# Attention and two feed-forward layers: the first batch pair in three full passes, opening loads in order of use, weights narrowed by an integer add

## The chip, the core and the metric

The kernel runs on one core of a Trainium2 chip. A core has five engines that run beside each other: TensorE (PE, matrix products; PEld is its weight load), VectorE (DVE), ScalarE (ACT), GpSimd (POOL) and SyncE (SP), which here issues all DMAs in order. The metric is the device time of one launch in microseconds.

## The reference

The inputs are eight batches of eight heads, 576 tokens, head size 64, and 32 packed queries per head; the weights come as 64-bit floats, which reach the kernel as pairs of 32-bit words.

```python
p_packed = sm_attn(p, k, v)               # 32 packed rows per head
out = sm_attn(q, p_packed, p_packed)      # every token against the 32 rows
x = out.transpose(0, 2, 1, 3).reshape(4608, 512)
xn = x / sqrt(mean(x * x) + 1e-6) * rms_g
x = (silu(xn @ w_gate) * (xn @ w_val)) @ w_out          # 1536 wide
h = x @ w_in
out = (max(h, 0) + alpha * min(h, 0)) @ w_out2          # 2048 wide
```

## The kernel before

**Products.** Every large product is made of three TensorE products of rounded parts (`mm3`, L107 to L110): high by high, high by low, low by high. The parts are made by `split_hi` on ScalarE (L96) and `split_lo` on VectorE (L99), or on GpSimd for output weights in later passes (L314).

**First feed-forward layer.** Its gate and value weights are folded with the packed values of a batch: `wg_job(b, j)` (L649) makes for batch b the folded weights of 256 hidden columns, six jobs a batch. A pass takes one chunk of tokens through the hidden blocks f of 128 columns: `blk_in` for gate and value (12 products per cut of the chunk between batches, two times six), silu (L886), product (L892), split (`hsplit`), then one step later `blk_out` (12 products into four PSUM banks that hold y). At the end of the pass y goes to DRAM (L930, L931).

**Chunks.** Batches 2 to 7 are taken in pairs: 320 tokens, 512 tokens (256 of either batch), 320 tokens. Batches 0 and 1 are taken in chunks of 320, 256, 320 and 256, and the two of batch 0 in half passes: first half of the blocks for both chunks, then second half, with partial y written out (`part`), reloaded (L874) and added (L923). Each half pass and each pass is an entry of `PASSES`; `NEWQ` and `XNEXT` say which chunk's queries are worked on and taken over in it.

**Narrowing.** The weights of the first layer are 36 units: 24 of gate and value columns, 12 of output rows, half a megabyte each. A unit is loaded wide by SP (L194 four DMAs, L199 one), then narrowed from 64 to 32 bits by `narrow`: shift and mask (L213, VectorE), sign and exponent bits (L220, VectorE), the low word as a float scaled by 2^-52 (L218, ScalarE), the exponent alone (L224, VectorE), their product (L228, GpSimd, or L231 on VectorE), and a float add (L239, GpSimd, or L237 on VectorE for the second layer's units, which `conv_late` narrows during the later passes). Narrowed gate and value units are also written to DRAM (L250), from where later batches reload them (L637). Eight wide buffers serve the first 18 units, four the rest. The generator `conv_all` narrows two units at a time; `conv` takes some of its steps and `conv_to(n)` takes all up to unit n.

**Attention.** `k_steps(b)` is the key chain of a batch: 11 TensorE steps, with evacuations between, that end in the packed values (`ppbd`, `ppB`, `ppG`). `q_steps` takes up to 256 query tokens: transposes (L537), scores (L553), softmax on VectorE and ScalarE (L564 to L583), a product whose squares give the norm (L590, L599), the power on GpSimd (L604), and the scaling (L613). Its scores need `ppB` of the batch. `x_split` makes the parts xh and xl that `blk_in` reads.

**Order.** The kernel writes the order of every engine's work by hand. In a step f: gate block, `work(f, 1)`, value block, `work(f, 2)`, `burst(f)`, `work(f, 3)`, then `blk_out(f - 1)` and the split of the next output weights. `burst` has four slots: folding jobs listed in `JOBS` take two each, key and query chains take what their step says. `work` runs the chains' evacuations; softmax steps with an exponential only at the third place, with table loads around (L353). In the passes of batch 0 and the half passes `work` also takes two narrowing steps; in later passes it takes steps of `conv_late`. At the end of a pass all steps of the next chunk's queries that are left are issued in one go, ahead of the last two `blk_out`. The prologue (from L664 on) loads keys and values, then weights and queries, runs the first key chain and the first query chains, narrows four units and folds the first job.

Of the kernel before, what the change touches and what calls it, by code (L numbers as in the profile page):

```python
# [18 lines left out]
def attention_moe_moe2_kernel(ctx, tc, q, k, v, p, w_gate, w_val, w_out, rms_g, w_in2, w_out2, alpha, out):  # L19
# [19 lines left out]
    NQ = 3  # L39
# [4 lines left out]
    CH = [(0, 320, [(0, 320, 0)]), (320, 256, [(0, 256, 0)]), (576, 320, [(0, 320, 1)]), (896, 256, [(0, 256, 1)])]  # L44
    for b in range(2, B, 2):
        t0 = b * S
        CH.append((t0, 320, [(0, 320, b)]))
        CH.append((t0 + 320, 512, [(0, 256, b), (256, 512, b + 1)]))
        CH.append((t0 + 832, 320, [(0, 320, b + 1)]))
    tiles, of_chunk = [], []  # L50
    for t0, n, _ in CH:
        ids = []
        for o in range(0, n, 128):
            ids.append(len(tiles))
            tiles.append((t0 + o, min(128, n - o)))
        of_chunk.append([ids[i:i + 2] for i in range(0, len(ids), 2)])
    HF = NF // 2
    PASSES = [(0, 0, HF), (1, 0, HF), (0, HF, NF), (1, HF, NF)] + [(c, 0, NF) for c in range(2, len(CH))]

    NEWQ = {0: 1, 2: 2, 4: 3, 5: 4}  # L60
    XNEXT = {0: 1, 3: 2, 4: 3, 5: 4}
    JOBS = {0: {1: [(0, 1)], 3: [(0, 2)]}, 1: {5: [(0, 3)]}, 2: {7: [(0, 4)], 9: [(0, 5)]}, 3: {11: [(1, 0)]},
            4: {2 * j + 1: [(1, j + 1)] for j in range(5)}, 5: {2 * j + 1: [(2, j)] for j in range(6)}}
    for i in range(6, len(PASSES)):
        b = 2 + (i - 6) // 3 * 2
        if i < len(PASSES) - 1:
            NEWQ[i] = XNEXT[i] = i - 1
        if (i - 6) % 3 == 0:
            JOBS[i] = {11: [(b + 1, 0)]}
        elif (i - 6) % 3 == 1:  # L70
# [41 lines left out]
    with tc.manual_schedule():  # L112
# [96 lines left out]
        def narrow(t, w, pool, late=False):  # L209
            lo, hi = t[:, :, :, 0], t[:, :, :, 1]  # L210
            wi = w.bitcast(I32)
            r = lo.bitcast(F32)
# [4 lines left out]
            if pool:  # L217
                nc.scalar.activation(out=r, in_=lo.bitcast(U32), func=ACTF.Copy, scale=2.0 ** -52)  # L218
# [4 lines left out]
            yield  # L223
            nc.vector.tensor_scalar(  # L224
                out=hi, in0=wi, scalar1=-0x800000, scalar2=None, op0=ALU.bitwise_and
            )
            if pool:
                nc.gpsimd.tensor_tensor(out=r, in0=r, in1=hi.bitcast(F32), op=ALU.mult)  # L228
            else:
                yield  # L230
                nc.vector.scalar_tensor_tensor(  # L231
                    out=r, in0=lo.bitcast(U32), scalar=2.0 ** -52, in1=hi.bitcast(F32),
                    op0=ALU.mult, op1=ALU.mult,
                )
            if late:
                yield
                nc.vector.tensor_tensor(out=w, in0=w, in1=r, op=ALU.add)  # L237
            else:
                nc.gpsimd.tensor_tensor(out=w, in0=w, in1=r, op=ALU.add)  # L239

        def conv_unit(n, pool):
# [5 lines left out]
            yield from narrow(staged.pop(n), w, pool)  # L247
# [5 lines left out]
        def conv_late():  # L253
            ahead = [load_wide(u, one, NST) for u in units2[:2]]
            for i, u in enumerate(units2):
                w = one.tile([128, 4, 128], F32, tag="w32", name="w32", bufs=2)
                yield from narrow(ahead.pop(0), w, 0, True)
# [16 lines left out]
        def conv_all():  # L274
            while n_conv[0] < NU1:
# [4 lines left out]
                live = [conv_unit(n, 1), conv_unit(n + 1, 1 if n % 3 else 0)]  # L280
# [62 lines left out]
        q_open = {b: sum(tiles[ids[0]][0] // S == b for c in of_chunk for ids in c) for b in range(B)}  # L343
# [281 lines left out]
        def new_x():  # L625
            return (one.tile([128, G, S], F32R, tag="xh", name="xh"),
                    one.tile([128, G, S], F32R, tag="xl", name="xl"))
# [71 lines left out]
        nc.sync.dma_start(out=g_col.rearrange("p (c o) -> p c o", o=1)[0:D], in_=rms_g[0:256].rearrange("(c d o) -> d c o", d=D, o=1))  # L699
        nc.sync.dma_start(out=g_col.rearrange("p (c o) -> p c o", o=1)[D:2 * D], in_=rms_g[256:512].rearrange("(c d o) -> d c o", d=D, o=1))  # L700
# [7 lines left out]
        nc.sync.dma_start(out=alpha_sb, in_=alpha.rearrange("(f p) -> p f", p=128))  # L708
        qa.run()
        warmup(3)  # L710
        qb = Chain(q_steps((2,), bk_pro), 0)
        qb.run()
        conv(1)
        warmup(3)
        qb.run()
        conv(1)
        qa.run()
        warmup(3)
        qb.run()
# [4 lines left out]
        qb.run()  # L724
# [3 lines left out]
        for i in range(2):  # L728
            x_split(of_chunk[0][i], xh, xl, i * 256)
# [44 lines left out]

        for i_p, (c, f0, f1) in enumerate(PASSES):
            last = i_p == len(PASSES) - 1
            t0, n, cuts = CH[c]
            xo = 320 * (c == 1)
            steady[0] = i_p > 3
            if i_p == 1:  # L780
                chains["k"] = [Chain(k_steps(b, bk_at), b) for b in range(1, B)]
# [240 lines left out]
```

## Time and profile before

| | us |
|---|---|
| median of 3 runs | 1797.76 (1795.12 to 1803.67) |
| the profiled execution | 1799.78 |
| its span, first to last instruction | 1798.0 |
| TensorE busy | 1680.2 (93%) |
| VectorE busy | 1112.8 (62%) |
| ScalarE busy | 820.4 (46%) |
| GpSimd busy | 282.2 (16%) |

The profile takes one execution apart. Busy times are sums per engine; TensorE's products are pipelined, so their durations overlap and the distance from start to start says more than the duration of one. The ends of the passes can be read from the instructions that take y out of PSUM: 135.0, 169.6, 210.0 and 246.3 us for the half passes, 318.5 and 384.5 for the two chunks of batch 1, then 451.1, 537.9 and 604.1 for the next pair. The second feed-forward layer begins at about 994.

### The profile page before, as it was taken

How to read it: one execution, taken by the hardware profiler on the slowest of the kernel's cores; microseconds unless marked ns; L12 is line 12 of the kernel's file. 1: busy time of each engine (PE TensorE's matmuls, PEld its weight loads, DVE VectorE, ACT ScalarE, POOL GpSimd, SP SyncE). 2: the span in 40 equal slices, each digit the busy share in tenths (PEclk: the TensorE clock that was granted, in tenths of full speed). 3: DMA queues.
4: the chain of work that ended last, by engine and by line, in shares of the span. 5: the costliest groups of instructions: out<-in, count | busy, mean ns of one | idle time of the engine just before them, and what ended most of it. 6: DMA issues, size and time to landing. Idle time of an engine off the chain costs nothing.

```text
span 1798.0 us, 27195 instructions
## 1 busy us (share of the span) xinstructions
PE 1680.2 (93%) x10448; PEld 1390.7 (77%) x10448; DVE 1112.8 (62%) x1945; ACT 820.4 (46%) x1564; POOL 282.2 (16%) x232
## 2 busy tenths in 40 slices
PE   6567879889999899999999999999999999999999
PEld 5256658678887798888889788888888888888887
DVE  3797747666646765566533666666666666666665
ACT  3236556666547655465545333333333333333332
POOL 1654202222222222233223000000000000000000
PEclk7779989999999999999999999999999999999999
DMA  8736636663545543443206101010101010100000
GB/s 191 211 124 191 184 105 188 178 184 92 145 140 156 159 121 114 141 154 100 91 24 229 68 1 48 1 48 0 48 0 48 0 48 0 47 1 24 1 24 24
DMA packets 163426, 164.05 MB, mean 91 GB/s; under 512 B 88544, under 2 KB 110048, under 8 KB 163296
## 3 DMA queue, kind: packets, MB, share of 16 engines
q1 hardware_dynamic: 163296, 162.32, 30.1%
q8 instruction: 82, 1.34, 0.3%
q14 instruction: 48, 0.39, 0.1%
HBM read 127.54 MB, written 34.73 MB: 90 GB/s over the span
## 4 chain that ended last, share of the span: by engine, by line
PE 78%; DVE 7%; ACT 7%; DMA 2%; issue 2%; SPq 1%; POOL 1%; DVEq 0%; ACTq 0%; POOLq 0%
PE ps_y L108 12%; PE ps_y L109 12%; PE ps_y L110 12%; PE ps_g L109 10%; PE ps_g L110 10%; PE ps_g L108 10%; PE ps_v L108 2%; PE ps_v L110 2%; PE ps_v L109 2%; PE ps_wg L649 2%; PE ps_at L590 1%; ACT L353 1%; DVE s L892 1%; ACT in_h L96 1%; ACT hh L96 1%
## 5 line engine op out<-in xcount | busy, mean ns | idle before, releaser
L96 ACT ACTIVATE hh<-s2m 128x512 fp32r<-128x512 f32 x144 | 91.1, 633 | 495.8 <-DVE s2m L975 495.8
L96 ACT ACTIVATE in_h<-w_raw 128x512 fp32r<-128x512 f32 x354 | 221.5, 626 | 113.1 <-PE ps_y L109 96.5
L314 POOL TENSOR_TENSOR in_l<-w_raw,in_h 128x512 fp32r<-128x512 f32 x131 | 177.9, 1358 | 559.1 <-ACT in_h L96 498.6
L109 PE MATMUL ps_g<-yl,in_h 128*128 128x512 f32 x576 | 228.0, 396 | 0.0
L110 PE MATMUL ps_y<-in_h,hl 128*128 128x512 f32 x576 | 226.9, 394 | 0.0
L109 PE MATMUL ps_y<-in_l,hh 128*128 128x512 f32 x576 | 226.8, 394 | 0.0
L110 PE MATMUL ps_g<-yh,in_l 128*128 128x512 f32 x576 | 226.4, 393 | 0.0
L108 PE MATMUL ps_y<-in_h,hh 128*128 128x512 f32 x576 | 225.7, 392 | 0.0
L108 PE MATMUL ps_g<-yh,in_h 128*128 128x512 f32 x576 | 225.3, 391 | 0.0
L108 PE MATMUL ps_y<-hh,in_h 128*128 128x320 f32 (+2 forms) x624 | 218.3, 350 | 2.2 <-ACT hh L96 2.2
L972 DVE TENSOR_SCALAR s2m<-ps_g,alpha_sb 128x512 f32<-128x512 f32 x144 | 108.0, 750 | 165.6 <-PE ps_g L110 165.6
L892 DVE TENSOR_TENSOR s<-s,ps_v 128x320 f32<-128x320 f32 (+2 forms) x156 | 81.2, 521 | 203.5 <-PE ps_v L110 136.0
L109 PE MATMUL ps_y<-hl,in_h 128*128 128x320 f32 (+2 forms) x624 | 205.6, 329 | 0.0
L110 PE MATMUL ps_y<-hh,in_l 128*128 128x320 f32 (+2 forms) x624 | 205.1, 329 | 0.0
L96 ACT ACTIVATE hh<-s 128x320 fp32r<-128x320 f32 (+2 forms) x156 | 78.0, 500 | 214.6 <-DVE s L892 214.6
L99 DVE TENSOR_TENSOR in_l<-w_raw,in_h 128x512 fp32r<-128x512 f32 x223 | 156.7, 716 | 24.1 <-ACT in_h L96 24.1
L99 DVE TENSOR_TENSOR hl<-s2m,hh 128x512 fp32r<-128x512 f32 x144 | 99.7, 693 | 109.2 <-ACT hh L96 109.2
L108 PEld LDWEIGHTS ps_y<-hh,in_h 128*128 128x128 f32 x624 | 120.8, 194 | 31.9 <-issue 22.4
L99 DVE TENSOR_TENSOR hl<-s,hh 128x320 fp32r<-128x320 f32 (+2 forms) x156 | 83.1, 532 | 88.3 <-ACT hh L96 88.3
L108 PE MATMUL ps_g<-xh,wgh 128*128 128x320 f32 (+1 forms) x384 | 117.7, 306 | 18.7 <-ACT E L404 6.9
L109 PEld LDWEIGHTS ps_g<-yl,in_h 128*128 128x128 f32 x576 | 108.1, 188 | 26.1
L108 PEld LDWEIGHTS ps_g<-yh,in_h 128*128 128x128 f32 x576 | 108.3, 188 | 25.7
(153 smaller groups left out, 3327.1 us busy)
## 6 DMA issues: line engine op xcount, KB each, us to landing
gv_raw<-gv_dram SPq DMA_DIRECT2D x168, 256.0 KB, 3.7
w<-in_moe_w_out_dram SPq DMA_DIRECT2D x28, 512.0 KB, 4.7
kt<-in_k_dram SPq DMA_DIRECT2D x64, 144.0 KB, 3.7
vt<-in_v_dram SPq DMA_DIRECT2D x16, 576.0 KB, 5.5
y_raw<-y_dram SPq DMA_DIRECT2D x9, 1024.0 KB, 6.1
qt<-in_q_dram SPq DMA_DIRECT2D x64, 128.0 KB, 3.8
w<-in_moe_w_in_dram SPq DMA_DIRECT2D x16, 512.0 KB, 4.3
w_dram<-w SPq DMA_DIRECT2D x32, 256.0 KB, 2.3
```

The source lines that it names most:

```text
L96: nc.scalar.activation(out=hi, in_=src, func=ACTF.Copy)
L99: nc.vector.tensor_tensor(out=lo, in0=src, in1=hi.bitcast(F32), op=ALU.subtract)
L108: nc.tensor.matmul(out=o, lhsT=lh, rhs=rh, start=first, stop=False)
L109: nc.tensor.matmul(out=o, lhsT=lh, rhs=rl, start=False, stop=False)
L110: nc.tensor.matmul(out=o, lhsT=ll, rhs=rh, start=False, stop=last)
L314: nc.gpsimd.tensor_tensor(out=l, in0=raw[u], in1=h.bitcast(F32), op=ALU.subtract)
L353: nc.scalar.activation(out=tick[0], in_=mhalf, func=func)
L590: nc.tensor.matmul(out=t[:, g * 256:(g + 1) * 256], lhsT=AT[:, g, k_ * rw:(k_ + 1) * rw], rhs=ppbd[par][:, :, g, :], start=True, stop=True,)
L649: nc.tensor.matmul(out=ts[g][h * NP:(h + 1) * NP, :], lhsT=ppG[b][g * D:(g + 1) * D, h, :], rhs=us[h][g * D:(g + 1) * D, :], start=True, s ...
L892: nc.vector.tensor_tensor(out=s, in0=s, in1=tv, op=ALU.mult)
L972: nc.vector.tensor_scalar(out=s, in0=t, scalar1=0.0, scalar2=alpha_sb[:, f:f + 1], op0=ALU.min, op1=ALU.mult)
```

## The change

Batches 0 and 1 become three chunks like the later pairs: 512 tokens of batch 0; 64 tokens of batch 0 and 256 of batch 1; 320 tokens of batch 1. Each is one full pass; the half passes, the partial y and the tables `PASSES`, `NEWQ` and `XNEXT` go. The first pass has all six jobs of batch 0 and the first of batch 1, all 36 units are narrowed by its end, and the key chains of batches 1 and on begin in it. In the first two passes `burst` serves the key chain ahead of the queries. In the prologue the loads go in the order four query loads (two tiles), four units, the other two tiles, four units, and the first narrowing steps come after the first key chain. `narrow` has four operations: the two VectorE ones as before, the low word scaled by 2^-29 and rounded to an integer on ScalarE, and an integer add on GpSimd; the units of the second layer are narrowed in the same way, in steps taken once per f or every second f.

```diff
-    CH = [(0, 320, [(0, 320, 0)]), (320, 256, [(0, 256, 0)]), (576, 320, [(0, 320, 1)]), (896, 256, [(0, 256, 1)])]
+        sizes = ([512], [64, 256], [320]) if b == 0 else ([320], [256, 256], [320])
...
-    PASSES = [(0, 0, HF), (1, 0, HF), (0, HF, NF), (1, HF, NF)] + [(c, 0, NF) for c in range(2, len(CH))]
...
+            if i == 0:
+                JOBS[i].update({2 * j + 1: [(0, j + 1)] for j in range(5)})
...
-            if pool:
-                nc.scalar.activation(out=r, in_=lo.bitcast(U32), func=ACTF.Copy, scale=2.0 ** -52)
+            nc.scalar.activation(out=lo, in_=lo.bitcast(U32), func=ACTF.Copy, scale=2.0 ** -29)
             yield
             nc.vector.scalar_tensor_tensor(
                 out=wi, in0=hi, scalar=-0x40000000, in1=wi, op0=ALU.bitwise_and, op1=ALU.bitwise_or
             )
-            yield
-            nc.vector.tensor_scalar(
-                out=hi, in0=wi, scalar1=-0x800000, scalar2=None, op0=ALU.bitwise_and
-            )
-            if pool:
-                nc.gpsimd.tensor_tensor(out=r, in0=r, in1=hi.bitcast(F32), op=ALU.mult)
...
-                nc.gpsimd.tensor_tensor(out=w, in0=w, in1=r, op=ALU.add)
+            nc.gpsimd.tensor_tensor(out=wi, in0=wi, in1=lo, op=ALU.add)
...
+        nc.sync.dma_start(out=g_col.rearrange("p (c o) -> p c o", o=1)[0:D], in_=rms_g[0:256].rearrange("(c d o) -> d c o", d=D, o=1))
+        nc.sync.dma_start(out=g_col.rearrange("p (c o) -> p c o", o=1)[D:2 * D], in_=rms_g[256:512].rearrange("(c d o) -> d c o", d=D, o=1))
         ck.run(2)
         warmup(4)
-        loads_to(1)
-        for i in range(NQ):
+        for i in range(2):
             load_q(i)
-        loads_to(9)
+        loads_to(4)
+        for i in range(2, NQ):
+            load_q(i)
+        loads_to(8)
         for n in range(9):
             ck.run()
-            if n == 5:
+            if n == 7:
                 qa.run()
-            if n in (4, 6):
-                conv(2)
...
-                if i_p < 4:
+                if c == 0:
                     conv(2)
-                elif not last and (at == 3 or at == 1 and f % 2 == 0):
+                elif not last and at == 3 and (f % 2 or n == T):
                     next(late, None)
...
-                k_turn(q_turn(free))
+                q_turn(f, k_turn(f, free)) if c < 2 else k_turn(f, q_turn(f, free))
...
+                if c == 0:
                     j1 = (f + 1) // 2
-                    conv_to(min(6 * j1 + (5 if f % 2 else 6), 18 if i_p == 0 else NU1))
+                    conv_to(min(6 * j1 + (5 if f % 2 else 6), NU1))
```

## Rows read from the trace of the kernel before

**Rows 1.** Windows: stretch, length, PE, PEld, DVE, ACT, POOL busy, PEclk, DMA share, GB/s

```profile
0.00:58.00 58.00, 36.77 (x288) 23.91 (x288) 23.84 (x60) 17.36 (x42) 12.40 (x19) 0.79 0.84 191
58.00:135.00 77.00, 47.21 (x203) 33.97 (x204) 69.33 (x99) 27.34 (x50) 47.39 (x37) 0.71 0.53 163
135.00:169.60 34.60, 27.07 (x207) 24.35 (x206) 27.48 (x46) 21.35 (x49) 16.59 (x13) 0.90 0.73 212
169.60:210.00 40.40, 33.26 (x322) 27.51 (x321) 29.78 (x57) 20.53 (x46) 14.85 (x11) 0.96 0.64 189
210.00:246.30 36.30, 29.75 (x243) 24.86 (x243) 21.93 (x58) 24.40 (x52) 1.25 (x2) 1.00 0.34 94
246.30:318.50 72.20, 62.63 (x547) 52.23 (x546) 42.59 (x90) 39.89 (x81) 15.40 (x12) 0.93 0.59 169
318.50:384.50 66.00, 59.11 (x602) 47.29 (x601) 43.72 (x101) 44.22 (x93) 17.43 (x14) 1.00 0.59 174
384.50:451.10 66.60, 60.47 (x528) 54.24 (x528) 42.66 (x91) 40.75 (x89) 18.44 (x15) 1.00 0.47 129
```

**Rows 2.** Timeline of PE: start us, length us, line, out<-in, count; several stretches

```profile
520.60 0.39 PE L110 MATMUL ps_y<-hh,in_l 128*128 128x512 f32 x1
...
522.87 0.28 PE L108 MATMUL ps_g<-xh,wgh 128*128 128x256 f32 x1
...
525.62 0.28 PE L110 MATMUL ps_v<-xh,wgl 128*128 128x256 f32 x1
...
316.21 0.31 PE L109 MATMUL ps_y<-hl,in_h 128*128 128x320 f32 x1
...
319.43 0.31 PE L110 MATMUL ps_y<-hh,in_l 128*128 128x320 f32 x1
...
206.41 0.46 PE L537 MATMUL ps_at<-ident,qt 64*128 64x64 f32 x4
```

**Rows 3.** Groups of DVE by form, 58 to 210 us: count | busy us, mean ns | idle before

```profile
L213 DVE TENSOR_SCALAR gv_raw<-w 128x512 int32<-128x512 int32 x20 | 17.5, 899 | 0.0
L220 DVE SCALAR_TENSOR_TENSOR gv_raw<-w,gv_raw 128x512 int32<-128x512 int32 x20 | 15.1, 778 | 0.0
L213 DVE TENSOR_SCALAR w_raw<-w 128x512 int32<-128x512 int32 x11 | 12.3, 1144 | 0.0
L220 DVE SCALAR_TENSOR_TENSOR w_raw<-w,w_raw 128x512 int32<-128x512 int32 x12 | 10.9, 932 | 0.0
L224 DVE TENSOR_SCALAR w<-gv_raw 128x512 int32<-128x512 int32 x20 | 10.5, 549 | 0.0
...
L224 DVE TENSOR_SCALAR w<-w_raw 128x512 int32<-128x512 int32 x12 | 5.5, 486 | 0.0
L231 DVE SCALAR_TENSOR_TENSOR w<-w 128x512 f32<-128x512 uint32 x5 | 5.2, 1050 | 0.1
```

**Rows 4.** Line L213, 58 to 247 us: count: shortest/median/longest ns, first to last start

```profile
L213 DVE TENSOR_SCALAR w_raw<-w x11: 411/1259/1524, 58.8 to 188.6; 128x512 int32<-128x512 int32 x11
```

**Rows 5.** Timeline of SP around 164 us

```profile
163.71 1.23 SPq L194 DMA_DIRECT2D w<-in_moe_w_val_dram  x2
```

**Rows 6.** Line L239, 58 to 247 us

```profile
L239 POOL TENSOR_TENSOR w_raw<-w_raw,w x12: 1283/1360/1634, 62.4 to 197.4; 128x512 f32<-128x512 f32 x12
```

**Rows 7.** Groups by form of the whole run

```profile
L537 PE MATMUL ps_at<-ident,qt 64*128 64x64 f32 x32 | 3.9, 246 | 0.0
...
L892 DVE TENSOR_TENSOR s<-s,ps_v 128x512 f32<-128x512 f32 x36 | 24.8, 688 | 87.3 <-PE ps_v L110 76.0 <-ACT s L886 11.2
...
L237 DVE TENSOR_TENSOR w<-w,w 128x512 f32<-128x512 f32 x32 | 26.1, 817 | 0.1
```

**Rows 8.** Timeline of all engines at the scores, the scaling and the first large product

```profile
31.49 0.63 PE L553 MATMUL ps_y<-qT,ppB 64*32 64x256 f32 x1 [0.42 <-ACT ppB L103]
...
45.72 0.67 DVE L613 TENSOR_TENSOR A2T<-A2T,ps_at 128x512 f32<-128x512 f32 x1
...
58.00 0.41 PE L108 MATMUL ps_g<-xh,wgh 128*128 128x320 f32 x1 [1.89 <-ACT xh L96]
```

More of the change, by code (lines that the diff above doesn't have):

```diff
@@ L222, in narrow, with conv_unit @@
             )
[L223 to L241 removed]
+            nc.gpsimd.tensor_tensor(out=wi, in0=wi, in1=lo, op=ALU.add)
+        def conv_unit(n):
             if n == NU1 // 2:
@@ L256, in conv_late @@
                 w = one.tile([128, 4, 128], F32, tag="w32", name="w32", bufs=2)
-                yield from narrow(ahead.pop(0), w, 0, True)
+                yield from narrow(ahead.pop(0), w)
                 nc.sync.dma_start(out=w_dram[i], in_=w)
@@ L342, in attention_moe_moe2_kernel @@
         chains = {"k": [], "q": []}
-        q_open = {b: sum(tiles[ids[0]][0] // S == b for c in of_chunk for ids in c) for b in range(B)}
+        q_open = {b: sum(tiles[ids[0]][0] // S == b for c in of_chunk for ids, _ in c) for b in range(B)}
         def need_k(b):
@@ L773, in y_at @@
             return y_dram[d:d + 2, :, t0:t0 + n].rearrange("d p t -> p d t")
[L775 to L780, printed above, removed]
+        for c, (t0, n, cuts) in enumerate(CH):
+            last = c == NP1 - 1
+            steady[0] = c > 0
+            if c == 0:
                 chains["k"] = [Chain(k_steps(b, bk_at), b) for b in range(1, B)]
-            if i_p in NEWQ:
-                chains["q"] = [Chain(q_steps(ids, bk_at), tiles[ids[0]][0] // S) for ids in of_chunk[NEWQ[i_p]]]
-            nq = of_chunk[XNEXT[i_p]] if i_p in XNEXT else []
+            nq = [] if last else of_chunk[c + 1]
+            chains["q"] = [Chain(q_steps(ids, bk_at), tiles[ids[0]][0] // S) for ids, _ in nq]
             first = [None]
@@ L801, in work @@
                             break
-                        ch.last = (i_p, f, at)
+                        ch.last = (c, f, at)
                         ch.next()
@@ L827, in q_turn, with burst @@
                         ch.next()
-                    return free
-                def k_turn(free):
-                    for ch in [ch for ch in chains["k"] if ch.kind is not None][:1]:
-                        if ch.done >= 7 and q_open.get(ch.b - 2) or ch.done == 10 and n_job[0] < NJ * (ch.b - 1):
-                            pass
-                        elif 0 < ch.kind <= free and ch.last != (i_p, f, 2):
-                            if free == 4:
-                                first[0] = ch
-                            free -= ch.kind
-                            ch.next()
-                    return free
-                k_turn(q_turn(free))
+                return free
+            def burst(f):
+                free = 4
+                for jb in JOBS[c].get(f, ()):
+                    wg_job(*jb)
+                    free -= 2
+                first[0] = None
+                q_turn(f, k_turn(f, free)) if c < 2 else k_turn(f, q_turn(f, free))
             ybk = [bank(f"y{d}")[:, 0:n] for d in range(KD)]
@@ L914, in attention_moe_moe2_kernel @@
             else:
-                both(("o", PASSES[i_p + 1][1]))
-                if len(nq) > 1:
-                    x_split(nq[1], xh, xl, off + 256)
-            blk_out(f1 - 1)
+                both(("o", 0))
+                for ids, o in nq[1:]:
+                    x_split(ids, xh, xl, o)
+            blk_out(NF - 1)
             for d in range(0, KD, 2):
-                if part:
-                    stg = part[d // 2]
-                    for i in range(2):
-                        nc.vector.tensor_tensor(out=stg[:, i], in0=stg[:, i], in1=ybk[d + i], op=ALU.add)
-                else:
-                    if i_p < 2:
-                        stg = ap.tile([128, 2, 320], F32, tag="part", name="part", bufs=2)[:, :, 0:n]
-                    else:
-                        stg = one.tile([128, 2, T], F32, tag="w64", name="stg", bufs=NST)[:, :, 0:n]
-                    for i in range(2):
-                        nc.scalar.activation(out=stg[:, i], in_=ybk[d + i], func=ACTF.Copy)
+                stg = one.tile([128, 2, T], F32, tag="w64", name="stg", bufs=NST)[:, :, 0:n]
+                for i in range(2):
+                    nc.scalar.activation(out=stg[:, i], in_=ybk[d + i], func=ACTF.Copy)
                 nc.sync.dma_start(out=y_at(c, d), in_=stg)
-            if i_p == len(PASSES) - 2:
+            if c == NP1 - 2:
                 ap_ctx.close()
```

138 lines of the change are left out of this document (65 added, 73 removed).

## The prediction

> **What bounds the kernel now.** I read the busy times by stretch first, cut at the ends of the token passes [rows 1]. The reader is to see that only the opening is loose. TensorE is busy 47.2 of 77 us in the stretch 58 to 135 at a granted clock of 0.71 (a mix of the two levels, 1.2 and 2.4 GHz), while VectorE is busy 69.3 of 77; from 135 to 210 TensorE has 60.3 of 75; from 384.5 on it has 91% of a pass at clock 1.00. Two chunks of batch 0, cut into four half passes, and two of batch 1 end at 384.5 us. The bare products of those passes need far less. Start-to-start distances at full clock are 0.227 us for 512 columns (520.60 to 522.87, ten steps), 0.1465 for 320 (22 steps) and 0.120 for 256 (23 steps) [rows 2]. With 576 products of 320 and 576 of 256 that is 84.4 + 69.1 = 153.5 us. The rest of the 384.5 is prologue (58), attention and weight folding, and waiting.
>
> Second, the VectorE groups of 58 to 210 [rows 3]: the seven rows of the narrowing sum to 77.0 us of the 126.6 that VectorE is busy there [rows 1], so 49.6 us are everything else. The shift-and-mask of L213 lasts 0.41 us at its shortest [rows 4]; here its means are 0.90 and 1.14 [rows 3], in the stretch in which GpSimd is busy 47 of 77 us. Third, the loads: the last gate/value load of the first weights is issued at 163.7 [rows 5], GpSimd's last narrowing add on output weights starts at 197.4 [rows 6]. So the 31 units left at 58 us take 139 us, 4.5 us each, and VectorE is what they wait on most of that time; the loads stand still meanwhile (163 GB/s against 212 in the next stretch).
>
> **The change, part by part.** *Passes.* Removed: four half passes and two chunks, with 576 products of 320 columns and 576 of 256. Added: 288 of 512, 432 of 320, and, in the chunk that spans both batches, 144 of 64 and 144 of 256. By [rows 2]: 65.4 + 63.3 + 17.3 = 146.0, plus the 64-column ones, a size that no row shows with these operands. The straight line through the three sizes gives 0.04; four 64-column transposes against 128 stationary columns stand (0.46 - 0.246)/3 = 0.07 apart [rows 2, 7]; more than the 0.120 of 256 columns is excluded since less is streamed. I take 0.08, next to the transposes: 11.5 us, ends 5.8 and 17.3. TensorE's own work goes from 153.5 to 157.5 (151.8 to 163.3): nothing is gained there. The Trainium skill (TensorE: Matmul & The Clock Gate, LDWEIGHTS) says a weight load of 128 columns takes about 128/1.2 = 107 ns however little is streamed; by it the 64-column products would cost 15.4 us and the change 3.9 more than I take, inside my ends; no row of before decides it.
>
> So the gain must come from the waiting. After the change the order is: prologue, one pass of 512 tokens during which all 36 units are narrowed, then two passes of 320.
>
> *Prologue.* Before, the narrowing's first VectorE steps stand between the steps of the attention chain, and a unit's load is issued ahead of the q tiles, so that the chain waits for weights. Now four q loads come first, then four units, then the other q tiles and four more units; the chain runs to its end before the first narrowing step. The two 0.6 us issues of g_col move ahead of the second v load on SP; nothing else queues there. On the other side the second q group grows from 64 to 256 tokens, whose score-to-scale chain takes 31.49 to 45.72, 14.2 us [rows 8], partly beside the first. First product at 58.00 [rows 8]; I take 51, ends 46 and 58.
>
> *The 512 pass.* Each step f needs three units. VectorE: a unit loses L224 (0.52) and in five cases L231 (1.05) [rows 3]; L213 and L220 stay. With one GpSimd operation for two I put L213 halfway between its shortest and its mean (0.41 and 0.96: 0.69) and leave L220 at 0.81: 1.5 for both. Some 30 units over 12 steps: 3.7 us per step. The rest is 49.6 us over 18 steps, 2.8, plus 0.4, an estimate, for the product and split that grow from 320 or 256 columns to 512 (0.688 there [rows 7]): 3.2. Sum 6.9. TensorE: 24 x 0.227 = 5.4, plus folding and attention, which in a 320 pass cost 66.6 - 288 x 0.1465 = 24.4 us [rows 1, 2], 2.0 a step: 7.5 at clock 1.00, about 10 at 0.75. Loads: before, 58 x 0.191 + 77 x 0.163 + 30 x 0.212 = 30.0 MB had moved by the last load [rows 1]; 0.7 MB of partial y (two tiles of 128 x 640 words) fall away. Of 29.3 MB, 11.1 are done by 58; the rest at 0.19, between those rates, takes 96 us, to 154 instead of 164. So VectorE stops being last; what is late next is TensorE at a mixed clock and the loads, both near 10 us a step. Twelve steps: 120, from 51 to 171 (ends 8 and 12.4 a step).
>
> The added wait stands at the end of this pass. Batch 1's key chain has 11 steps, now all inside this pass, one per f; its last is at f = 10, and at f = 11 the folding job and the next batch's key chain take all four slots. The 256 query tokens of batch 1 in the next chunk can't start before; the pass's closing loop runs their whole chain in one go. Queued behind it on TensorE are the last two output blocks (24 x 0.227 = 5.4 us). By the same stretch as above, 14.2 us at a low clock with other work between [rows 8], I take 13; ends 10 and 17. Pass end: 171 + 13 + 5.4 = 189.4, where before had finished its third half pass at 210.
>
> *The two 320 passes.* Products: 144 x (0.1465 + 0.120 + 0.08) = 49.9, and 42.2. Folding and attention add 24.4 as above: 74.3 + 66.6 = 140.9 (ends 125 and 155; the 320 pass at 246.3 took 72.2). Pair end 330 instead of 384.5: 54.5 saved. Partial sums (eight adds, four reloads) go with the half passes.
>
> *Later passes.* A late unit loses three VectorE operations, of which L237 alone is 32 x 0.82 = 26 us [rows 7], and gains one on ScalarE and one on GpSimd (1.36 by [rows 6]); its steps now come once or half as often per f. TensorE is idle 6.1 of 66.6 in such a pass [rows 1], and VectorE is not what ends most of it. I take 4 us saved in all, ends 15 saved and 6 lost (ScalarE now waits for a unit's load in the row of silu and splits; cover is that two loads are ahead).
>
> *Sum* against the profiled execution, 1799.8 (span 1798.0 and 1.8 around it): 1799.8 - 54.5 - 4 = 1741.3. The median of the runs shown lies 2.0 lower: **1739**.
>
> **The rivals.** *(a) The pace of narrowing doesn't change*, because what held it was its place in the queues, not VectorE's work: GpSimd's adds hold the write of each unit, and SP the loads behind it. For it: loads at 163 GB/s while VectorE was full may be SP waiting on GpSimd. Then the last add is 7 us earlier, 190; f = 11, the wait and the last blocks follow: 190 + 10 + 13 + 5.4 = 218, pair end 359, 1797.8 - 25.5 - 4 = 1768. *(b) Better than forecast*: the clock rises early and steps take 8 us: 51 + 96 + 18.4 = 165, passes at 130, pair end 295, 1797.8 - 89.5 - 6 = 1702. For it: VectorE's 6.9 and TensorE's 7.5; against: loads would have to sustain 29.3 - 9.7 = 19.6 MB in some 90 us, 0.22. *(c) Slower than before, by the integer add.* No row shows a GpSimd integer add; float adds take 1.36 [rows 6]. Three adds per step: the pass reaches before's pair end when 12 steps take 384.5 - 140.9 - 18.4 - 51 = 174 us, 14.5 a step, 4.8 per add. At 7 us per add the pass takes 252, and the time is 1797.8 + 78 - 4 = 1872. Against it: same tile, same operands in number and stride. The Trainium skill (GPSIMD Engine Reference, When to use GPSIMD) says such an all-int32 add is native to the cores; that speaks for a price near the float add, and no row here shows it.
>
> **How the numbers follow.** Forecast 0.55 (1715 to 1760), (a) 0.22, (b) 0.13, (c) 0.05, and 0.05 for small losses (long wait, ScalarE held by late loads) that leave it near 1790 or above. Range 1700 to 1775: it reaches (a) and (b) and leaves out (c), the small losses and the far ends. Half a per cent, 9 us, is about what a measurement of this kernel can tell from no change. Faster by more: 0.55 + 0.22 + 0.13 less a little of (a), 0.88; within: 0.05; slower: 0.07.
>
> **What would show it.** In the profile after: first product near 51; the 512 pass ending near 190 with VectorE well under 85% busy in it; a TensorE gap of 10 to 17 us at its end, on the scores and scales of the next chunk; 64-column products 0.04 to 0.12 apart; the integer add near 1.4 us; the third pass ending near 330; the later passes within a few us of their old lengths. Wrong: VectorE still full in the first pass, an add of 3 us or more, a first pass that ends after 210, or later passes that change by over 10 us in sum.

## The result, and the profile after

The changed kernel takes 1753.74 us (median of 4 runs, 1750.11 to 1755.27) against 1797.68 for the kernel before: a ratio of 0.9748, 95% interval 0.9719 to 0.9777. It is 44 us faster; 59 were forecast. The profiled execution took 1755.27, its span is 1753.3.

Windows of the changed kernel, cut near the ends of its passes (columns as in [rows 1]): prologue, first, second, third and fourth pass. The cut behind the second pass lies 1.2 us behind the pass end of the table further down, the next one 0.9 ahead of it.

```profile
0.00:51.40 51.40, 30.25 (x290) 21.72 (x290) 22.55 (x55) 19.53 (x46) 9.23 (x16) 0.85 0.81 190
51.40:189.40 138.00, 105.55 (x605) 73.20 (x606) 89.28 (x157) 71.16 (x131) 44.75 (x34) 0.87 0.70 203
189.40:279.20 89.80, 82.53 (x743) 72.12 (x742) 37.22 (x89) 50.88 (x103) 20.37 (x17) 0.92 0.53 152
279.20:345.70 66.50, 62.12 (x577) 51.61 (x575) 38.70 (x87) 45.89 (x94) 19.57 (x17) 1.00 0.56 163
345.70:410.30 64.60, 62.00 (x535) 55.09 (x536) 36.84 (x81) 45.24 (x95) 21.98 (x19) 1.00 0.44 118
```

VectorE, 90% busy from 58 to 135 before [rows 1], is busy 65% of the first pass now, and the DMAs move 203 GB/s where they moved 163. The third and the fourth pass run at clock 1.00. The odd row is the second pass: 90 us at clock 0.92 (88.6 by the table), where the third, with as many tokens, takes 66.5 (68.7).

Groups of VectorE in the first pass (51 to 189), the two operations that narrowing keeps:

```profile
L223 DVE SCALAR_TENSOR_TENSOR gv_raw<-w,gv_raw 128x512 int32<-128x512 int32 x20 | 15.5, 776 | 0.0
...
L217 DVE TENSOR_SCALAR gv_raw<-w 128x512 int32<-128x512 int32 x20 | 12.6, 629 | 10.8 <-DMA w<-in_moe_w_val_dram 10.5
L223 DVE SCALAR_TENSOR_TENSOR w_raw<-w,w_raw 128x512 int32<-128x512 int32 x12 | 9.5, 810 | 0.0
...
L217 DVE TENSOR_SCALAR w_raw<-w 128x512 int32<-128x512 int32 x11 | 5.4, 493 | 6.4 <-DMA w<-in_moe_w_out_dram 6.4
```

They sum to 43.0 us, where the seven rows of narrowing summed to 77.0 [rows 3]. VectorE now stands idle ahead of L217 because of loads, 16.9 us in all.

### The profile page after: what moved, and what is told of

It is laid out like the page before. It is cut to its first block, busy times and chain, and to the rows that moved or that the text cites. A ratio compares the mean times of both kernels' runs of the same rounds, so it can differ in the third digit from the quotient of the medians.

```text
span 1753.3 us, 26725 instructions
## 1 busy us (share of the span) xinstructions
PE 1666.4 (95%) x10298; PEld 1377.6 (79%) x10298; DVE 998.1 (57%) x1763; ACT 842.7 (48%) x1596; POOL 280.8 (16%) x234
## 4 chain that ended last, share of the span: by engine, by line
PE 82%; ACT 6%; DVE 4%; DMA 3%; SPq 1%; issue 1%; POOL 0%; ACTq 0%; DVEq 0%; POOLq 0%
PE ps_y L113 13%; PE ps_y L114 12%; PE ps_y L115 12%; PE ps_g L114 10%; PE ps_g L115 10%; PE ps_g L113 10%; PE ps_v L113 2%; PE ps_v L115 2%; PE ps_v L114 2%; PE ps_wg L636 2%; PE ps_at L577 2%; ACT L340 2%; DMA w<-in_moe_w_out_dram 1%; SPq L199 1%; DVE s L866 1%
## 5 line engine op out<-in xcount | busy, mean ns | idle before, releaser
L101 ACT ACTIVATE in_h<-w_raw 128x512 fp32r<-128x512 f32 x342 | 213.7, 625 | 102.8 <-PE ps_y L114 88.5
L301 POOL TENSOR_TENSOR in_l<-w_raw,in_h 128x512 fp32r<-128x512 f32 x131 | 170.5, 1302 | 394.3 <-ACT in_h L101 348.5
L866 DVE TENSOR_TENSOR s<-s,ps_v 128x320 f32<-128x320 f32 (+1 forms) x144 | 79.6, 553 | 263.4 <-PE ps_v L115 190.1
L113 PE MATMUL ps_y<-hh,in_h 128*128 128x320 f32 (+1 forms) x576 | 209.3, 363 | 2.2 <-ACT hh L101 2.2
L114 PE MATMUL ps_y<-hl,in_h 128*128 128x320 f32 (+1 forms) x576 | 197.1, 342 | 0.1
L115 PE MATMUL ps_y<-hh,in_l 128*128 128x320 f32 (+1 forms) x576 | 197.1, 342 | 0.0
L104 DVE TENSOR_TENSOR in_l<-w_raw,in_h 128x512 fp32r<-128x512 f32 x211 | 145.9, 706 | 12.6 <-ACT in_h L101 12.4
L101 ACT ACTIVATE hh<-s 128x320 fp32r<-128x320 f32 (+1 forms) x144 | 75.5, 524 | 148.3 <-DVE s L866 148.3
L113 PE MATMUL ps_g<-xh,wgh 128*128 128x256 f32 (+3 forms) x384 | 118.0, 307 | 16.0 <-ACT E L391 7.0
L104 DVE TENSOR_TENSOR hl<-s,hh 128x320 fp32r<-128x320 f32 (+1 forms) x144 | 82.5, 573 | 85.0 <-ACT hh L101 85.0
L113 PEld LDWEIGHTS ps_y<-hh,in_h 128*128 128x128 f32 x576 | 111.2, 193 | 23.2 <-issue 11.6
```

Of the source, the lines that this page charges most:

```text
L101: nc.scalar.activation(out=hi, in_=src, func=ACTF.Copy)
L104: nc.vector.tensor_tensor(out=lo, in0=src, in1=hi.bitcast(F32), op=ALU.subtract)
L113: nc.tensor.matmul(out=o, lhsT=lh, rhs=rh, start=first, stop=False)
L114: nc.tensor.matmul(out=o, lhsT=lh, rhs=rl, start=False, stop=False)
L115: nc.tensor.matmul(out=o, lhsT=ll, rhs=rh, start=False, stop=last)
L301: nc.gpsimd.tensor_tensor(out=l, in0=raw[u], in1=h.bitcast(F32), op=ALU.subtract)
```

## The experiments

The kernel before took 1797.7 to 1800.5 us (medians) beside these runs, so medians are compared to about 3 us. A second measure is taken from the traces: the *pass ends*, here the start of the first DMA that stores y.

| | first pass or 4th half pass | pair end | end of first layer | median |
|---|---|---|---|---|
| before | 246.1 | 385.5 | 993.8 | 1797.7 |
| after | 189.4 | 346.6 | 948.1 | 1753.7 |
| e1_float | 225.4 | 380.2 | 984.8 | 1792.9 |
| e2_before_int | 216.1 | 353.7 | 967.3 | 1770.0 |
| e3_open | 189.1 | 351.0 | 953.3 | 1755.2 |
| e5_onecut | 186.9 | 337.5 | 939.7 | 1745.9 |
| e4_fill | 182.4 | 338.1 | 940.1 | 1744.9 |
| e6_prime | 182.3 | 335.8 | 937.5 | 1746.0 |
| e7_fill_prime | 182.8 | 331.6 | 933.6 | 1741.8 |
| e8_skip | 174.3 | 332.0 | 933.4 | 1738.7 |
| e9_halfload | 174.7 | 332.3 | 934.2 | 1741.5 |
| e12_nowrite | 177.2 | 333.0 | 934.2 | 1746.4 |
| e10_qfirst | 185.9 | 332.4 | 942.6 | 1748.5 |
| e11_all | 185.1 | 326.0 | 935.4 | 1740.9 |

One caution on this table: eight of these kernels run the same instructions up to the last step of the first pass, and the time from the first silu to the last in it was 104.4 to 109.4 us (mean 107.5; the profiled run of after has the longest). A difference of 5 us in the first pass of two traces is therefore no finding by itself.

### Which part pays: the narrowing or the passes

e1_float puts the float narrowing of before, with its pacing, into the changed kernel:

```diff
-            nc.gpsimd.tensor_tensor(out=wi, in0=wi, in1=lo, op=ALU.add)
+            ... L224 to L239 of the kernel before
```

> The changed kernel with the float narrowing of before (five or six operations a unit, late units in five steps), everything else as changed. Theory 1 (VectorE's share of the narrowing held the first passes; with it gone the loads come last): VectorE goes from 89 us busy of 138 in the first pass to 110 or more, the first pass ends at 200 to 215 instead of 188, and with some 5 us in the later passes the time is 1770 to 1785. Theory 2 (the order of passes gave the gain, the narrowing's work was covered): the first pass still ends within 5 us of 188 and the time is 1753 to 1762.

Measured: 1792.85, ratio 0.9972 (0.9956 to 0.9989). The new passes without the new narrowing are nearly worth nothing. That is theory 1's direction, but above its range: the first pass ends 10 us later than it said. Window of its first pass from the first silu on, two groups of VectorE in it, and the longest wait of TensorE's weight loads:

```profile
69.60:225.40 155.80, 110.41 (x585) 72.74 (x586) 116.07 (x185) 64.01 (x122) 72.85 (x58) 0.84 0.52 154
```

```profile
L218 DVE TENSOR_SCALAR gv_raw<-w 128x512 int32<-128x512 int32 x19 | 15.9, 863 | 7.4 <-DMA w<-in_moe_w_val_dram 7.4
...
L218 DVE TENSOR_SCALAR w_raw<-w 128x512 int32<-128x512 int32 x10 | 11.0, 1137 | 0.0
```

```profile
PEld ps_wg L654 <- POOL gv_raw L244: 18.6, 10, 4.7
```

VectorE is back at 116 us in these 156, the DMAs fall to 154 GB/s, and the folding products wait for GpSimd's float add. The first product comes at 61.9, the pass ends at 225.4.

e2_before_int is the kernel before with the integer narrowing alone, its rarer steps for the late units included:

```diff
-            yield from narrow(staged.pop(n), w, pool)
+            yield from narrow(staged.pop(n), w)      # shift-mask, sign bits, scaled int, integer add
```

> The kernel before with the integer narrowing alone; half passes, opening and chunks as before. Theory 1: the third half pass ends at 185 to 197 instead of 210, the later passes give some 5 us, and the time is 1770 to 1782, half of the whole gain or nearly. Theory 2: the third half pass ends within 5 us of 210 and the time is 1788 to 1796.

Measured: 1769.98, ratio 0.9856 (0.984 to 0.9871). Its first large product, and its first half pass from 58 us on:

```profile
53.26 0.41 PE L108 MATMUL ps_g<-xh,wgh 128*128 128x320 f32 x1 [1.88 <-ACT xh L96]
```

```profile
58.00:119.70 61.70, 39.09 (x197) 29.52 (x196) 49.93 (x77) 30.78 (x57) 30.15 (x22) 0.75 0.77 242
```

The first product comes at 53.3 instead of 58.0, and from it the half pass lasts 66.4 us instead of 77 [rows 1], at 242 GB/s in the window instead of 163. The third half pass ends at 180, earlier than theory 1 said. At the pair end the two parts are: narrowing alone 385.5 - 353.7 = 31.8, passes and opening alone 5.3, both 38.9. So about four fifths of the gain up to there is the narrowing, in either pass plan. Behind the pair end it is the other way round. From there to the end of the first layer the plan of before takes 608.3 (before) and 613.6 (e2), the new one 604.6 (e1) and 601.5 (after). The 4 to 12 us of the later passes thus belong to the new plan.

### The opening

e3_open gives the changed kernel the opening of before: one unit's load ahead of all queries, g_col's loads behind them, narrowing steps within the key chain.

```diff
-        for i in range(2): load_q(i)
-        loads_to(4)
-        for i in range(2, NQ): load_q(i)
+        loads_to(1)
+        for i in range(NQ): load_q(i)
...
+            if n in (4, 6): conv(2)
```

> The changed kernel with the opening of before: one unit's load ahead of the queries, narrowing steps between the steps of the first key chain. First large product near 58 instead of 51.4. Theory A (the pass follows its start): the first pass ends 5 to 8 us later and the time is 1758 to 1762. Theory B (the loads set the pace of the first pass, whatever its start): the end of the first pass moves by less than 3 us and the time is 1750 to 1757.

Measured: 1755.16, ratio 0.9772 (0.975 to 0.9795); the changed kernel has 0.9748 (0.9719 to 0.9777). The first large product, in e3_open and then in the changed kernel:

```profile
56.50 0.49 PE L113 MATMUL ps_g<-xh,wgh 128*128 128x512 f32 x1 [2.37 <-ACT xh L101]
```

```profile
51.44 0.80 PE L113 MATMUL ps_g<-xh,wgh 128*128 128x512 f32 x1 [2.37 <-ACT xh L101]
```

5.1 us are won at the first product, and at the end of the pass of these two traces nothing is left of them: 189.1 and 189.4. By the caution above that is no finding by itself: from the first silu to the last it is 103.0 us in e3_open, and the 109.4 of the changed kernel is the longest of eight. The pair end of e3_open is 4.4 later, by a second pass of 93.3 us instead of 88.6 in which no instruction differs, which was not explained. In the medians the new opening is worth 1.4 us, which these runs can tell neither from zero nor from the 5.

### What paces the first pass now

e9_halfload loads half of each unit from unit 8 on and narrows that half twice; e12_nowrite drops the write of the narrowed gate and value units (later batches then read other data).

```diff
-                for i, w in enumerate((w_gate, w_val)):
+                for i, w in enumerate((w_gate, w_val)[:2 - short]):     # short: n >= 8
```

> The changed kernel; from unit 8 on only the first half of each wide unit is loaded (gate columns without value columns, half of the output columns) and narrowed twice, so the weights are wrong; the number of narrowing instructions stays, the scaled low words are written packed into the other half of the buffer. 28 units x 0.25 MB = 7 MB of the 28 MB that the first pass moves fall away, and two of four load issues of a gate/value unit. If the bytes of the loads set the 10 us a step: at the same 203 GB/s the pass loses up to 34 us, and stops at what TensorE needs, 7.5 to 8.5 us a step: first pass ends 165 to 172, in all 1754 - 20 = 1734 (1728 to 1740). If instead the order of the queues sets it (a load lands 3 to 5 us after its issue anyway, and its issue waits for a buffer or for a narrowed unit to write), the pass changes by under 5 us: 1749 to 1755.

```diff
-                nc.sync.dma_start(out=gv_dram[u[1]], in_=w.rearrange("p c x -> p (c x)"))
```

> The changed kernel without writing the narrowed gate and value units to DRAM; the reloads of the later batches read a piece of v of the same size instead, so their weights are wrong. 24 x 0.25 = 6.3 MB fall away in the first pass, and SP no longer waits for GpSimd's add in front of the next loads (8 waits, 13.7 us in the pass after the change). If the bytes set the pace: nearly as much as the half loads, 1754 - 18 = 1736. If SP's waits for the narrowed units set it: 1754 - 10 = 1744 (1740 to 1747), and the half loads bring little. If neither does (TensorE at its mixed clock and the order of steps): 1750 to 1755 for both.

Measured: 1741.48 for the half loads, ratio 0.9677 (0.966 to 0.9695), and 1746.42 without the writes, 0.9716 (0.9695 to 0.9738). The first lies between the two theories, nearer to the bytes; the second is in the range given to SP's waits, but by that theory the half loads should have brought little. Windows of steps 0 to 7 and of 8 to 11 in the changed kernel, then in e9_halfload:

```profile
51.40:146.30 94.90, 70.84 (x382) 47.93 (x383) 64.37 (x112) 54.27 (x99) 38.27 (x29) 0.88 0.80 230
146.30:168.00 21.70, 21.70 (x161) 16.18 (x167) 15.46 (x29) 9.32 (x19) 5.79 (x4) 1.00 0.77 236
```

```profile
51.40:133.20 81.80, 67.62 (x381) 45.52 (x381) 65.83 (x111) 52.68 (x99) 39.72 (x29) 0.92 0.61 181
133.20:155.00 21.80, 21.80 (x161) 16.30 (x167) 15.53 (x30) 9.35 (x18) 5.70 (x4) 1.00 0.73 212
```

The last steps are TensorE's in both: no idle time, clock 1.00, 7 us a step. Only the first eight get shorter. From the first silu to the last the pass takes 96.8 us with half loads and 99.0 without the writes, against 107.5 (mean of the eight): 10.7 us for 7 MB and 8.6 for 6.3 MB, 1.5 and 1.4 us per MB. Each is from one trace, and the traced run of e12_nowrite took 1740.0 us, 6.4 less than the median of its five, so its 1.4 is rather too high. At 203 GB/s a MB takes 4.9 us. So the transfers set a part of the pace, under a third of what that rate would give. They do so whether loads or writes are taken away, and e9 keeps the writes on which SP waits, so SP's waiting isn't needed to explain it. That it is their bytes isn't shown, since SP's time to issue them goes with them:

```profile
118.77 1.22 SPq L199 DMA_DIRECT2D w<-in_moe_w_gate_dram  x2
120.03 1.23 SPq L199 DMA_DIRECT2D w<-in_moe_w_val_dram  x2
```

A gate or value unit takes four issues of 0.6 us; the 72 such issues in steps 0 to 7 of the changed kernel take 43 of 95 us. e9_halfload drops half of them, e12_nowrite 22 writes of 0.4 us, and no run separates issues from bytes. The 9.6 us a step that e9 still takes there, with TensorE busy 67.6 of 81.8 and VectorE 65.8, were not taken apart further.

### The second pass

Three things stand out in its trace. TensorE's timeline at a gate block of the mixed chunk:

```profile
232.03 0.28 PE L113 MATMUL ps_g<-xh,wgh 128*128 128x64 f32 x1
232.15 0.28 PE L114 MATMUL ps_g<-xl,wgh 128*128 128x64 f32 x1
232.26 0.28 PE L115 MATMUL ps_g<-xh,wgl 128*128 128x64 f32 x1
232.37 0.36 PE L113 MATMUL ps_g<-xh,wgh 128*128 128x256 f32 x1
232.57 0.28 PE L114 MATMUL ps_g<-xl,wgh 128*128 128x256 f32 x1
232.69 0.28 PE L115 MATMUL ps_g<-xh,wgl 128*128 128x256 f32 x1
```

The 64-column products are 0.11 apart, and the first one of 256 columns behind them holds the next for 0.20. The twelve products of a block take 1.38 us (231.78 to 233.16), where 6 x 0.08 + 6 x 0.120 = 1.20 was forecast: 24 x 0.18 = 4.3 us in the pass.

SP's issue of the first late loads, ScalarE's scaling that waits for one, and TensorE behind it; then the waits at the end of the pass and the products after them:

```profile
200.27 0.38 SPq L204 DMA_DIRECT2D w<-in_moe_w_in_dram  x1
200.75 0.46 SPq L204 DMA_DIRECT2D w<-in_moe_w_out_dram  x1
```

```profile
206.55 0.68 ACT L221 ACTIVATE w<-w 128x512 int32<-128x512 uint32 x1 [2.39 <-DMA w<-in_moe_w_in_dram]
```

```profile
208.11 1.63 PE L540 MATMUL ps_at<-qT,ppB 64*32 64x256 f32 x16 [3.23 <-ACT s L860]
...
269.32 1.05 PE L577 MATMUL ps_at<-ppbd,A2T 128*64 128x256 f32 x4 [2.32 <-DVE A2T L570]
272.01 0.36 PE L596 MATMUL ps_at<-ident,s 64*128 64x64 f32 x1 [1.64 <-POOL s L591]
...
273.01 0.47 PE L115 MATMUL ps_y<-hh,in_l 128*128 128x320 f32 x1
273.27 0.47 PE L113 MATMUL ps_y<-hh,in_h 128*128 128x320 f32 x1
```

Windows of stretches of that pass:

```profile
201.00:211.00 10.00, 6.77 (x57) 5.43 (x56) 3.20 (x10) 5.10 (x12) 1.27 (x1) 0.77 0.64 216
211.00:221.00 10.00, 10.00 (x82) 9.03 (x81) 4.04 (x8) 3.63 (x7) 1.52 (x2) 0.89 0.27 84
221.00:261.00 40.00, 39.92 (x426) 34.72 (x425) 19.40 (x49) 23.50 (x48) 11.92 (x10) 1.00 0.65 178
261.00:279.20 18.20, 14.24 (x86) 13.29 (x86) 6.37 (x15) 9.70 (x21) 4.37 (x4) 0.81 0.29 83
```

Behind the wait near 208 and behind the closing waits the granted clock is at its lower level for a while (means of 0.77, 0.89 and 0.81 in these windows): the products after 272 are 0.267 apart instead of 0.1465, about 20 of them, 2.4 us.

e5_onecut takes gate and value of the mixed chunk in one cut of 320 columns with batch 0's weights:

```diff
-                for lo, hi, b in cuts:
+                for lo, hi, b in [(0, 320, 0)] if c == 1 else cuts:
```

> The changed kernel, but in the second pass all 320 tokens are multiplied with the folded weights of batch 0, in one cut, so that its gate and value products are 288 of... 144 of 320 columns instead of 144 of 64 and 144 of 256 (the values of 256 tokens are then those of other weights). Theory A (products bind the second pass, and a 64-column product costs 0.11 us as its trace shows): 144 x (0.111 + 0.120 - 0.1465) = 12 us less, the second pass takes 78 us instead of 90 and the time is 1740 to 1744. Theory B (the second pass waits on ScalarE and VectorE): under 5 us less, 1749 to 1754.

Measured: 1745.89, ratio 0.9723 (0.9708 to 0.9737). The second pass, by its ends, is 82.3 instead of 88.6 us. A block of 320 columns is 6 x 0.1465 = 0.88 against 1.38, so 12 us less for TensorE; it idles 12.9 us of the shorter pass (82.33 long, busy 69.42) where it idled 7.3, so half of what the cut costs is hidden by other waits.

e4_fill issues the last two output blocks between the steps of the next chunk's queries, e6_prime issues the first two late loads at the end of the first pass, e7_fill_prime does both, and e8_skip leaves the attention of batch 1's first 256 tokens out from the scores on:

```diff
+                        if ch.kind > 0 and ch.done >= 2 and pend:      # e4, e7
+                            blk_out(pend.pop(0))
                         ch.next()
...
             ahead = [load_wide(u, one, NST) for u in units2[:2]]
+            yield                                                      # e6, e7
...
+                elif c == 0:                                           # e6, e7
+                    next(late)
...
+            if tiles[ids[0]][0] == S:                                  # e8
...
+                return
```

> The changed kernel; in the closing loop of a pass the last two output blocks stand between the scores and the second product, and between that and the scaling, of the next chunk's queries, instead of behind all of it. Theory A (TensorE's wait at the end of the first and the second pass costs its length and the clock behind it): the gaps of 5.7, 1.8, 2.3 and 1.6 us are filled, fewer products run at the low clock, and the time falls by 8 to 14 us, to 1740 to 1746. Theory B (the chain of the queries itself is last, so that the blocks only move): the first pass's end moves by under 3 us and the time is 1750 to 1755.

> The changed kernel with the first two loads of the second layer's units issued at the end of the first pass, not in the step that narrows the first of them. Theory A (ScalarE, waiting in order for that load, holds the second pass): TensorE's wait of 3.2 us near 208 and some low-clock products after it go, 3 to 7 us less, 1747 to 1751. Theory B (covered): within 2 us of the changed kernel, 1752 to 1756.

> Both of the last two edits together. If they act on different waits their gains add: 11 to 20 us less than the changed kernel, 1734 to 1743. If one wait only hides the other, the time is that of the better of the two.

> The changed kernel without the attention of the first 256 tokens of batch 1 behind their transposes (scores, softmax, second product, norm and scaling are left out for these tokens; their values are the transposed queries). Theory A: the whole wait at the end of the first pass is worth its 12.5 us and the low clock behind it: 13 to 18 us less, the first pass ends at 171 to 175, 1736 to 1741. Theory B (something else, the loads or the first pass's own work, ends the first pass): under 6 us less, 1748 or above.

Measured: 1744.91, ratio 0.9686 (0.9661 to 0.9711); 1746.03, 0.97 (0.9674 to 0.9726); 1741.82, 0.9671 (0.965 to 0.9693); 1738.68, 0.9654 (0.9632 to 0.9676). From the first pass's last silu to its end: 22.9 us in after, 17.8 with the filling, 8.0 without the attention, with the last silu at 166.5 and 166.4 in after and e8. So the closing wait is worth 15 us with its own products. How much of it the filling takes is not settled: the same stretch is 19.5 in e7 and 20.8 in e11, which fill it too, and 20.9 to 22.7 in e5, e6 and e10, which don't. The early loads shorten the second pass from 88.6 (89.0 and 93.3 in e8 and e3, with the same instructions) to 85.0, filling and early loads together to 80.3 with the clock at 0.98. The medians of e4 and e6 are 9 and 8 below after's, both together 12: not the sum. Some of e6's gain lies in the first pass (182.3 against 189.4), up to whose last step its instructions are those of after; 5 us of that are within what those passes scatter, so the price of the late loads alone is known only as 4 to 8.

e10_qfirst gives the queries the first place in the second pass too, e11_all adds e7's edits:

```diff
-                q_turn(f, k_turn(f, free)) if c < 2 else k_turn(f, q_turn(f, free))
+                q_turn(f, k_turn(f, free)) if c < 1 else k_turn(f, q_turn(f, free))
```

> The changed kernel, with the key chain ahead of the queries in the first pass only; in the second pass the queries of the third chunk come first, as in all later passes. If the wait at the end of the second pass (266 to 272 us, then products at half clock) is the price of that priority: second pass shorter by 6 (4 to 10), 1754 - 6 = 1748. If the chain's evacuations or slots just move the wait to the key chain of the next batch pair (folding jobs of batch 2 late): no change, 1751 to 1757.

> The changed kernel with the last two output blocks issued between the steps of the next chunk's queries, the first two late loads issued at the end of the first pass, and the queries first in the second pass. The first two gave 1741.8 together. If the wait at the end of the second pass was still there with them, 1741.8 - 5 = 1737; if the filling had already covered it, 1741 to 1743.

Measured: 1748.52, ratio 0.972 (0.9698 to 0.9742), and 1740.87, 0.9676 (0.9659 to 0.9692). In e10 the second and the third pass are 6.2 and 4.5 us shorter, but from the pair end to the end of the first layer it takes 610.2 instead of 601.5. Its ninth pass, and that of the changed kernel:

```profile
702.03:766.43 64.40, 60.76 (x562) 50.95 (x562) 35.45 (x82) 42.74 (x87) 20.99 (x18) 1.00 0.52 164
```

```profile
714.52:772.50 57.98, 56.41 (x452) 48.42 (x451) 32.17 (x68) 37.93 (x78) 21.56 (x18) 1.00 0.60 182
```

TensorE is busy 4.4 us longer there: work that the priority had put earlier comes back in later passes. The gain that remains in e10 is 5 us, about the closing wait of the second pass and the clock behind it; with the filling (e11 against e7) it is 1 us, less than the runs can tell. e7 and e11 are the fastest kernels that compute all, 12 and 13 us under the change.

## Why the prediction was right, and where it was not

1739 was forecast, 1753.74 came; the profiled execution stands 14.0 above the sum of 1741.3.

**Narrowing and VectorE: right.** The mean of L217 was put at 0.69 and is 0.63 and 0.49; L223 was left at 0.81 and is 0.78 and 0.81. The integer add, of which no row told anything, has the price of the float add:

```profile
L226 POOL TENSOR_TENSOR gv_raw<-gv_raw,w x24: 1274/1292/1594, 29.7 to 150.2; 128x512 int32<-128x512 int32 x24
L226 POOL TENSOR_TENSOR w_raw<-w_raw,w x12: 1293/1418/1640, 53.5 to 155.4; 128x512 int32<-128x512 int32 x12
```

Medians of 1.29 and 1.42 us against 1.36 [rows 6]. Rival (c) needed 4.8. The Trainium skill (GPSIMD Engine Reference, When to use GPSIMD) calls such an add native to the cores; the trace's price fits that. Rival (a), an unchanged pace, would have ended the first pass at 218, and fell; in e2 the pace rose in the old plan too. Which part of the narrowing did it, VectorE's three operations less or GpSimd's one less, was not tried apart. The two are tied: in the trace VectorE's shift-and-mask waits for the GpSimd instruction that runs when it starts, and the wait counts as busy time of VectorE.

```profile
68.08 1.28 POOL L226 TENSOR_TENSOR gv_raw<-gv_raw,w 128x512 int32<-128x512 int32 x1 [1.28 <-DVE gv_raw L223]
68.45 1.20 DVE L217 TENSOR_SCALAR w_raw<-w 128x512 int32<-128x512 int32 x1 [0.50 <-DMA w<-in_moe_w_out_dram]
70.94 0.43 DVE L217 TENSOR_SCALAR w_raw<-w 128x512 int32<-128x512 int32 x1 [1.29 <-DMA w<-in_moe_w_out_dram]
```

In the first pass the 7 of 31 that start while a GpSimd instruction runs end 0.28 to 0.30 us behind its end (here 69.36 and 69.65); the other 24 take 0.38 to 0.43. In the kernel before, 18 of the 31 from 58 to 210 end so. So VectorE's 90% there held waits for GpSimd, and its 77.0 us of narrowing were not all its own work.

**First pass: right as a sum.** Twelve steps were to take 120 us. The silus start at 57.05 (f = 0), 138.64 (f = 7) and 166.48 (f = 11): 9.95 a step. But they are not alike: 11.7 for the first seven, 7.0 for the last four. Taking loads and clock as one rate of 10 hid that, so that the sum came out is partly luck. TensorE's own 7.5 at full clock was near the 7.0. The pass ends at 188.2 by the same reading as before; 189.4 was forecast.

**The wait at its end: right.** 13 us were forecast for it, on the scores and scales of the next chunk:

```profile
170.50 0.74 PE L540 MATMUL ps_at<-qT,ppB 64*32 64x256 f32 x16 [0.87 <-ACT pT L108]
176.95 3.78 PE L577 MATMUL ps_at<-ppbd,A2T 128*128 128x256 f32 x8 [5.71 <-DVE A2T L570]
182.55 0.69 PE L596 MATMUL ps_at<-ident,s 128*128 128x128 f32 x2 [1.81 <-POOL s L591]
182.89 0.78 PE L113 MATMUL ps_y<-hh,in_h 128*128 128x512 f32 x1
```

From 170.5 to 182.9 it is 12.4 us, and e8 shows that the pass gets 15 shorter without it.

**The opening: right at its place, its weight not shown.** 51 was forecast, 51.44 came. The order of loads and steps, to which the forecast put it, is a part of that: with the float narrowing the new order has its first product at 61.9 (e1), and the integer narrowing alone moves it to 53.3 in the old order (e2). The sum let those 7 us run through to the pass end. e3 gives no sign that they do: 1.4 us in the medians, with a first product 5 us later.

**The second pass: wrong, and the whole miss.** The step that failed is "folding and attention add 24.4 as above: 74.3". It took the extras of a settled 320 pass at clock 1.00 for a pass that follows the first. From the first instruction that takes y out of PSUM to the next pass's, the second pass took 88.5 us (188.2 to 276.7), 14.2 more. The waits are the smaller part of that: TensorE idles 7.3 us in it, and the 24.4 already held 6.1 of idle time. Its busy time is what grew, 81.3 us against 60.5 + 7.7 = 68.2 for the settled pass with the forecast's products, 13.1 more:

```profile
188.18:276.71 88.53, 81.26 (x736) 70.65 (x735) 36.99 (x91) 50.34 (x102) 19.38 (x17) 0.93 0.53 152
276.71:343.53 66.82, 63.38 (x582) 53.14 (x582) 37.67 (x86) 46.82 (x96) 18.91 (x16) 0.99 0.53 154
```

Of the 13.1 the 64-column cut takes 4.3. The folding takes as much: the second pass has five folding jobs, and the pass that the 24.4 was read from has one.

```profile
L649 PE MATMUL ps_wg<-gv_raw,ppG 64*32 64x512 f32 x16 | 1.1, 601 | 0.0
L636 PE MATMUL ps_wg<-gv_raw,ppG 64*32 64x512 f32 x80 | 5.4, 601 | 0.0
```

(First the kernel before, 384.5 to 451.1, then the changed one, 189.4 to 279.2.) The clock takes about 5, an estimate: by the windows its lower level lasted some 14 us, TensorE was busy in about 10 of them and did about half as much; 2.4 of the 5 are the slow products after 272. That is 13.6, so the account closes within its rounding. It tells where the time went, not what each part would give back: e5 got back half of the cut. The nearest row, the 320 pass of batch 1 at 246.3 with its five folding jobs, 72.2 us at clock 0.93 [rows 1], was used for the upper end alone; its extras of 30.0 would have given 79.9.

Two of the terms had been looked at and put aside. The 64-column product was taken by its nearest row, transposes 0.07 apart; it takes 0.11. The Trainium skill (TensorE: Matmul & The Clock Gate, LDWEIGHTS) gives the time of a weight load as its columns divided by 1.2, in ns, an estimated 107 ns for 128. The trace's 0.11 us from start to start agrees with that. And for ScalarE's wait for a unit's load the cover was said to be "two loads are ahead". For the first unit none is: the loads are issued at 200.27 and 200.75, at the generator's first step, and its scaling stands in ScalarE's queue at 206.55, ahead of a silu that TensorE waits on. The closing wait of the second pass, with the slow products behind it, was not named in the forecast.

**Third and later passes: right, partly by luck.** 66.8 (276.7 to 343.5) for 66.6, but TensorE is busy 63.4 of it instead of 60.5, with six folding jobs instead of one, and idles 3.4 instead of 6.1. Part of the 66.6 is a mixed reading: 384.5 is where y is first taken out of PSUM, 451.1 where its store is issued; by either reading alone that pass took 65.6 to 65.8. Later, 3.5 us were saved for 4 by the first reading and 5.7 by the second. The reason given, fewer VectorE operations, is not what the traces show: from the pair end on, with the float narrowing the new plan kept over half of what it saved (604.6 against 601.5 and 608.3), and integer narrowing in the old plan, with its rarer late steps, lost 5.

## What to carry to other kernels

When one engine is full, price its instructions one by one, see whether its busy time holds waits for another engine, and take the cheaper form first: here the narrowing without the new passes gave 28 us, and the new passes without the narrowing 5. Time saved ahead of a stretch that another resource paces need not be a gain (5 us at the first product could not be found again), so a sum should carry it only to the next point where something else ends last. And do not price the first pass of a new plan like a settled one: count the jobs in the row that the price is read from, ask of each stream what it finds already loaded at its first step, and add the stretch at a lower clock that followed TensorE's waits of 2 to 6 us here.

## What the runs showed of the hardware

- A product of 64 columns saves next to nothing over one of 256 with 128 x 128 weights: 0.11 against 0.120 us from start to start, and the first larger one behind a row of small ones takes 0.20.
- The same shift-and-mask on VectorE (128 x 512) took between 0.38 and 1.52 us in the first pass. Its means are 0.63 and 0.49 with GpSimd busy 32% of the time, and 0.86 and 1.14 in e1_float, with GpSimd busy 47%. All that last over 0.6 us, in both, start while a GpSimd instruction runs and end 0.28 to 0.30 us behind it.
- In the first pass, the same instructions took 104.4 to 109.4 us from first to last silu in eight traces, so such a stretch should be read from more than one of them.
